# First head pair side by side in the opening, with two dummy products fewer: a linear-attention and bilinear-FFN kernel

## Chip, cores, metric

One core of one Trainium2 chip. The metric is the device time of the whole kernel in microseconds (us); one launch computes everything. Runs of this kernel come out at 322 to 324 us.

## The reference

Batch 8, 8 heads, 576 tokens, head width 64. Attention without softmax, an RMS norm over each head's 64 outputs, then an FFN on 4608 tokens with two up-projections that are multiplied:

```python
kv  = np.einsum('bhsd,bhse->bhde', k, v)          # one 64x64 matrix per head
out = np.einsum('bhsd,bhde->bhse', q, kv)
rms = np.sqrt(np.mean(out * out, axis=-1, keepdims=True) + 1e-06)
x   = (out / rms * g_norm)                         # -> [4608, 512]
y   = ((x @ w_a) * (x @ w_b)) @ w_out              # d_ff = 1536
```

## The kernel before

Eight batches of attention are woven into the FFN's strips of 512 tokens. Only batch 0's attention has no FFN to hide under: it is the opening, and it runs while the first weights are still being loaded. Heads go in pairs: head 2p on partitions 0 to 63 and head 2p+1 on 64 to 127 of each result. The 576 tokens are laid on 96 partitions, six tokens each (`EP, EC = 96, 6`).

The helpers for one pair (cuts marked with `# ...`):

```python
def kv(self, p, o):                       # 12 products, K = 96, 64x64 each
    for c in range(EC):
        for j in range(2):
            nc.tensor.matmul(
                o[j * D : (j + 1) * D, :],
                lhsT=kt[self.b % NB][:, 2 * p + j, c, :],
                rhs=vt[self.b % NB][:, 2 * p + j, c, :],
                start=(c == 0), stop=(c == EC - 1))

def qtr(self, p, i):                      # 12 transposes, 64 columns of weights each
    t = P[:, i, :].bitcast(BF16)[:, 0:S].rearrange("q (c t) -> q c t", c=EC)
    for c in range(EC):
        for j in range(2):
            nc.tensor.transpose(t[j * D : (j + 1) * D, c, :],
                                qt[self.b][:, 2 * p + j, c, :], ident[0:EP, 0:EP])
```

The opening. `dummy(n, i)` issues n products of zeros, 128x512, whose results nobody reads: they keep TensorE busy while the inputs land.

```python
A = Attn(0)
nc.vector.tensor_copy(qt[0][:, 0:2], q32)         # casts fp32 -> bf16 of the first pair
nc.scalar.copy(kt[0][:, 0:2], k32)
nc.vector.tensor_copy(vt[0][:, 0], v32[:, 0])
nc.scalar.copy(vt[0][:, 1], v32[:, 1])
dummy(11, 0)
A.qtr(0, 2); A.qtr_out(0, 2)                      # transposes of q, copy to SBUF
dummy(4, 7)
A.kv1(0, SS)                                      # the 12 products of kv
A.kv1_out(0, SS, nc.vector.tensor_copy)           # one 128x64 copy, PSUM -> kvs
A.qtr(1, 3); A.qtr_out(1, 3)                      # the second pair's transposes
nc.tensor.matmul(P[:, 1, 0:1], lhsT=g_row, rhs=one, start=True, stop=True)
# ...
A.px(0, X[0])                                     # q times kv, first pair
# ... the other pairs, then the first FFN products:
u0.first((0, 1))                                  # w_a, then w_b, of the first half of d_model
```

## Time and profile before

| | kernel before |
|---|---|
| time, three runs | 322.81, 323.08, 323.35 us |
| the profiled run | 324.26 us, span on the core 322.5 us |
| PE busy | 315.1 us, 98% of the span |
| opening on PE, first transposes to the first FFN product | 5.78 to 14.05 us |
| PE waits for the first piece of w_b | 1.05 us, until 15.71 us |
| PE waits for v of batch 2 | 1.00 us, until 61.20 us |

How to read the lines: the line numbers are those of the kernel; most are of helpers. In the kernel before L312 is a dummy, L164 a transpose, L140 a kv product, L178 `px`, L237 an FFN up-projection. In the changed kernel each of these is four higher, and L368, L372 and L381 are the new transposes, kv products and kvs copies. In e9 to e11 below each is one higher than before (L141, L238).

Busy time from the page of the kernel before (engine, us, share of the span, instructions):

```profile
PE 315.1 (98%) x1945; PEld 151.1 (47%) x1945; DVE 123.6 (38%) x214; ACT 125.3 (39%) x216; POOL 60.2 (19%) x82
```

PE's timeline in the opening of the kernel before (start us, duration us, engine, line, operation, weights' size, result size, count; in brackets the idle time ahead of it and what ended that):

```profile
5.78 0.45 PE L164 MATMUL P<-ident,qt 96*64 96x96 bf16 x12 [0.28 <-DVE qt L353]
6.16 1.04 PE L312 MATMUL P<-zeros 128*128 128x512 bf16 x4
7.13 0.38 PE L140 MATMUL P<-vt,kt 96*64 96x64 bf16 x12
7.34 0.42 PE L164 MATMUL P<-ident,qt 96*64 96x96 bf16 x12
7.69 0.38 PE L365 MATMUL P<-one,g_row 1*128 1x1 f32 x2
8.00 0.43 PE L178 MATMUL P<-qT,kvs 64*64 64x288 bf16 x4
...
14.05 0.60 PE L237 MATMUL P<-xt,wa_t 128*128 128x512 bf16 x2
15.71 0.60 PE L237 MATMUL P<-xt,wb_t 128*128 128x512 bf16 x2 [1.05 <-DMA wb_t<-in_moe_w_b_dram]
```

The 12 transposes, four dummies and 12 kv products follow each other from 5.78 us; the second pair's transposes start at 7.34 us. PE is done with the attention and the first two w_a products at 14.65 us and then has nothing to do until the first piece of w_b lands.

The second half of the cast of v, from ScalarE's timeline of the same run; it ends at 6.87 us, and kv of the second head can't begin before:

```profile
6.36 0.51 ACT L356 CAST vt<-v 96x384 bf16<-96x384 f32 x1
```

Two lines of PE's waits over the whole span (who waited for what: us in total, times, longest):

```profile
PE P L237 <- DMA wb_t<-in_moe_w_b_dram: 1.1, 1, 1.1
PE P L140 <- DMA vt<-in_v_dram: 1.0, 1, 1.0
```

And the second of them in the timeline, batch 2's 48 kv products:

```profile
61.20 0.95 PE L140 MATMUL P<-vt,kt 96*64 96x64 bf16 x48 [1.00 <-DMA vt<-in_v_dram]
```

### The profile page before, as it was taken

To read this page: it belongs to the slowest core of one execution; us is meant where nothing else is said; L and a number is where in the kernel's file an instruction comes from. 1 tells how busy PE (TensorE), PEld (TensorE's weight loads), DVE (VectorE), ACT (ScalarE), POOL (GpSimd) and SP (SyncE) were. 2 spreads that over 40 slices of the span, in tenths; PEclk is the share of its full clock that TensorE was granted. 3 is DMA by queue.
4 is the path that set the end of the run, shared out by engine and by line. 5 is a ranking of instruction groups with operands and counts; after the bars stand their busy time and mean duration, and the time that the engine had idled before them with its cause. 6 is when DMAs were issued, how large, how long until landed. Compare 5 with 4: busy or idle time off the path is not lost.

```text
span 322.5 us, 4835 instructions
## 1 busy us (share of the span) xinstructions
PE 315.1 (98%) x1945; PEld 151.1 (47%) x1945; DVE 123.6 (38%) x214; ACT 125.3 (39%) x216; POOL 60.2 (19%) x82
## 2 busy tenths in 40 slices
PE   8799999899999999999999999999999999999995
PEld 3344454444444444444444445444444444444443
DVE  3544335344244432543244333532355233313421
ACT  3542255354335434552355325533464233123310
POOL 8864870140032150320050000000000000000000
PEclk9999999999999999999999999999999999999999
DMA  8999999997359999496597142003000200020002
GB/s 180 197 196 200 192 173 236 140 116 117 91 103 151 143 143 226 57 154 131 138 102 122 52 97 56 2 33 99 2 0 0 100 33 0 17 95 23 0 35 98
DMA packets 69901, 32.61 MB, mean 101 GB/s; under 512 B 43638, under 2 KB 65398, under 8 KB 69878
## 3 DMA queue, kind: packets, MB, share of 16 engines
q0 software_dynamic: 49712, 18.44, 48.5%
q1 hardware_dynamic: 19810, 13.44, 16.8%
q10 hardware_dynamic: 356, 0.43, 0.4%
q8 instruction: 15, 0.25, 0.3%
q14 instruction: 8, 0.07, 0.1%
HBM read 37.75 MB, written 12.98 MB: 157 GB/s over the span
## 4 chain that ended last, share of the span: by engine, by line
PE 80%; DMA 14%; POOL 4%; issue 1%; ACT 0%; POOLq 0%
PE P L237 49%; PE P L287 26%; DMA wb_t<-in_moe_w_b_dram 6%; DMA vt<-in_v_dram 5%; PE P L217 2%; PE P L191 2%; DMA wo_t<-in_moe_w_out_dram 2%; PE P L140 2%; DMA qt<-in_q_dram 2%; POOL qs L122 1%; POOL kt L99 1%; POOL vt L99 1%; POOL qt L99 1%; POOL wa_t L340 0%; POOL wb_t L340 0%
## 5 line engine op out<-in xcount | busy, mean ns | idle before, releaser
L255 DVE TENSOR_TENSOR ab<-P,asb 128x512 bf16<-128x512 f32 x108 | 74.5, 692 | 125.4 <-PE P L237 124.4
L237 PE MATMUL P<-xt,wb_t 128*128 128x512 bf16 x432 | 111.7, 379 | 1.1 <-DMA wb_t<-in_moe_w_b_dram 1.1
L237 PE MATMUL P<-xt,wa_t 128*128 128x512 bf16 x432 | 111.9, 379 | 0.0
L287 PE MATMUL P<-wo_t,ab 128*128 128x512 bf16 (+1 forms) x444 | 97.9, 373 | 0.0
L251 ACT CAST asb<-P 128x512 bf16<-128x512 f32 x108 | 63.0, 585 | 81.8 <-PE P L237 80.3
L237 PEld LDWEIGHTS <-wb_t 128*128 128x128 bf16 x432 | 42.2, 98 | 52.2 <-DMA wb_t<-in_moe_w_b_dram 1.5
L287 PEld LDWEIGHTS <-ab 128*128 128x128 bf16 x444 | 43.1, 98 | 45.6
L237 PEld LDWEIGHTS <-wa_t 128*128 128x128 bf16 x432 | 41.7, 98 | 44.5 <-issue 0.5
L205 DVE SCALAR_TENSOR_TENSOR xt<-P,g_col,rs 128x288 bf16<-128x288 f32 x64 | 30.1, 513 | 25.4 <-ACT rs L195 25.4
L195 ACT ACTIVATE rs<-P,eps_t 128x576 f32<-128x576 f32 (+1 forms) x33 | 23.9, 726 | 22.4 <-PE P L191 18.4
L300 ACT COPY osb<-P 128x512 f32<-128x512 f32 x17 | 9.9, 585 | 48.6 <-PE P L287 46.8
L187 ACT ACTIVATE sq<-P 128x576 bf16<-128x576 f32 x31 | 20.1, 650 | 19.9 <-PE P L217 18.0
L302 DVE COPY osb<-P 128x512 f32<-128x512 f32 x18 | 12.5, 692 | 32.4 <-PE P L287 32.3
L122 POOL DMA_DIRECT2D qs<-in_q_dram x12 | 19.6, 1633 | 2.0 <-issue 1.9
L119 POOL COPY gate<-qT 1x1 bf16<-1x1 bf16 x5 | 0.9, 176 | 92.8 <-DMA qT<-qs 92.8
L191 PE MATMUL P<-sq,ones 128*128 128x288 bf16 x64 | 13.2, 286 | 0.5 <-ACT sq L187 0.4
L217 PE MATMUL P<-qT,kvb 128*128 128x288 bf16 x56 | 11.7, 286 | 0.0
L151 ACT CAST kvb<-P 64x256 bf16<-64x256 f32 (+1 forms) x20 | 6.0, 301 | 12.9 <-PE P L140 12.8
L191 PEld LDWEIGHTS <-ones 128*128 128x128 bf16 x64 | 6.2, 98 | 7.4 <-issue 0.4
L140 PE MATMUL P<-vt,kt 96*64 96x64 bf16 x384 | 8.6, 197 | 1.0 <-DMA vt<-in_v_dram 1.0
L140 PEld LDWEIGHTS <-kt 96*64 96x64 bf16 x384 | 7.3, 112 | 4.8 <-issue 4.4
L99 POOL DMA_DIRECT2D vt<-in_v_dram x13 | 9.1, 698 | 0.5 <-DMA qt<-in_q_dram 0.5
(41 smaller groups left out, 65.9 us busy)
## 6 DMA issues: line engine op xcount, KB each, us to landing
out_dram<-osb SPq DMA_DIRECT2D x23, 256.0 KB, 2.0
qs<-in_q_dram POOLq DMA_DIRECT2D x12, 288.0 KB, 6.4
kt<-in_k_dram POOLq DMA_DIRECT2D x6, 576.0 KB, 8.4
vt<-in_v_dram POOLq DMA_DIRECT2D x6, 576.0 KB, 11.1
out_dram<-osb SPq DMA_DIRECT2D x13, 128.0 KB, 2.3
wo_t<-in_moe_w_out_dram POOLq DMA_DIRECT2D x12, 128.0 KB, 6.0
wa_t<-in_moe_w_a_dram POOLq DMA_DIRECT2D x5, 256.0 KB, 9.1
wb_t<-in_moe_w_b_dram POOLq DMA_DIRECT2D x5, 256.0 KB, 8.8
```

The costliest lines, as they stand in the source:

```text
L99: nc.gpsimd.dma_start(out=t[:, hs, :, :], in_=src[b, hs].rearrange("h (t c) d -> t h c d", c=EC))
L122: nc.gpsimd.dma_start(out=d[:, hs, :], in_=q[b, hs].rearrange("h t d -> t h d"))
L140: nc.tensor.matmul(o[j * D : (j + 1) * D, :], lhsT=kt[self.b % NB][:, 2 * p + j, c, :], rhs=vt[self.b % NB][:, 2 * p + j, c, :], start=(c ...
L187: nc.scalar.activation(sq[p % 3], P[:, i0 : i0 + 2, 0:HF], AF.Square)
L191: nc.tensor.matmul(P[:, i0 + h, 0:HF], lhsT=ones, rhs=sq[p % 3][:, h, :], start=True, stop=True)
L195: nc.scalar.activation(rs[p % 3][:, h0:h1, :], P[:, i0 + h0 : i0 + h1, 0:HF], AF.Abs_reciprocal_sqrt, bias=eps_t,)
L205: nc.vector.scalar_tensor_tensor(out=xt[p][:, t0 : t0 + HF], in0=P[:, x0 + h, 0:HF], scalar=g_col, in1=rs[p % 3][:, h, :], op0=ALU.mult, o ...
L217: nc.tensor.matmul(P[:, i0 + h, 0:HF], lhsT=kvb[self.b % 2][:, p, :], rhs=self.qT[:, p, h * HF : (h + 1) * HF], start=True, stop=True,)
L237: nc.tensor.matmul(self.a if w is wa_t else self.b, lhsT=w[:, kc, self.fc * 128 : (self.fc + 1) * 128], rhs=xt[kc][:, t0 : t0 + STRIP], st ...
L251: nc.scalar.copy(self.t, self.a)
L255: nc.vector.tensor_mul(abt[self.s % 2][self.fc], self.b, self.t)
L287: nc.tensor.matmul(P[:, i, e0:e1], lhsT=abt[s % 2][fc][:, g * 128 : (g + 1) * 128], rhs=wo_t[:, fc, e0:e1], start=(fc == 0), stop=(fc == F ...
```

## The change

The intent: with the two heads side by side in the free dimension, one transpose and one kv product serve both heads, six instead of twelve of each, and two dummies that seem not to be needed are dropped. kv then yields a 128x128 result, of which only the two diagonal 64x64 blocks are wanted, so the copy to `kvs` becomes two copies.

```diff
+    qc = sb([EP, EC, 2 * D], BF16, "qc")
+    kc0 = sb([EP, EC, 2 * D], BF16, "kc0")
+    vc = sb([EP, EC, 2 * D], BF16, "vc")
 ...
-    nc.vector.tensor_copy(qt[0][:, 0:2], q32)
-    nc.scalar.copy(kt[0][:, 0:2], k32)
-    nc.vector.tensor_copy(vt[0][:, 0], v32[:, 0])
-    nc.scalar.copy(vt[0][:, 1], v32[:, 1])
-    dummy(11, 0)
-    A.qtr(0, 2)
+    nc.vector.tensor_copy(by_token(qc), q32)      # by_token: "p c (h d) -> p h c d"
+    nc.scalar.copy(by_token(kc0), k32)
+    nc.vector.tensor_copy(by_token(vc)[:, 0], v32[:, 0])
+    nc.scalar.copy(by_token(vc)[:, 1], v32[:, 1])
+    dummy(10, 0)
+    t = P[:, 2, :].bitcast(BF16)[:, 0:S].rearrange("q (c t) -> q c t", c=EC)
+    for c in range(EC):
+        nc.tensor.transpose(t[:, c, :], qc[:, c, :], ident[0:EP, 0:EP])
     A.qtr_out(0, 2)
-    dummy(4, 7)
-    A.kv1(0, SS)
-    A.kv1_out(0, SS, nc.vector.tensor_copy)
+    dummy(3, 7)
+    for c in range(EC):
+        nc.tensor.matmul(P[:, SS, 0 : 2 * D], lhsT=kc0[:, c, :], rhs=vc[:, c, :],
+                         start=(c == 0), stop=(c == EC - 1))
+    for j in range(2):
+        r = slice(j * D, (j + 1) * D)
+        nc.vector.tensor_copy(A.kvs[r, 0, :], P[r, SS, r])
```

More of the change, by code (lines that the diff above doesn't have):

```diff
@@ L352, with by_token @@
     A = Attn(0)
-    nc.vector.tensor_copy(qt[0][:, 0:2], q32)
-    nc.scalar.copy(kt[0][:, 0:2], k32)
-    nc.vector.tensor_copy(vt[0][:, 0], v32[:, 0])
-    nc.scalar.copy(vt[0][:, 1], v32[:, 1])
-    dummy(11, 0)
-    A.qtr(0, 2)
-    A.qtr_out(0, 2)
-    dummy(4, 7)
-    A.kv1(0, SS)
-    A.kv1_out(0, SS, nc.vector.tensor_copy)
+    def by_token(t):
+        return t.rearrange("p c (h d) -> p h c d", h=2)
+    nc.vector.tensor_copy(by_token(qc), q32)
[6 more added lines that the diff above has]
+        nc.tensor.transpose(t[:, c, :], qc[:, c, :], ident[0:EP, 0:EP])
+    A.qtr_out(0, 2)
+    dummy(3, 7)
+    for c in range(EC):
+        nc.tensor.matmul(
+            P[:, SS, 0 : 2 * D],
+            lhsT=kc0[:, c, :],
+            rhs=vc[:, c, :],
+            start=(c == 0),
+            stop=(c == EC - 1),
+        )
+    for j in range(2):
+        r = slice(j * D, (j + 1) * D)
+        nc.vector.tensor_copy(A.kvs[r, 0, :], P[r, SS, r])
     A.qtr(1, 3)
```

## The prediction

> **What bounds the kernel now.** TensorE. The page shows PE busy 98% of a 322.5 us span; from about 16 us on, the chain of waits is almost only FFN products (75% of the span on two lines). The change touches only the opening. In the timeline, PE waits for the cast of q until 5.78 us, runs batch 0's attention until 14.65 us, then idles 1.05 us, until 15.71 us, for the first piece of w_b (view of waits: "PE <- DMA wb_t 1.1, 1 time"). POOL issued that piece at 8.55 us. The stretches table shows the DMA engines saturated from 4 us on (about 200 GB/s), and POOL's issues depend on nothing that PE computes. After 15.71 us PE has no wait of note. So 15.71 us is set by transfers, not by the attention.
>
> **What the change does, costed.**
> - First pair's transposes: 12 of 64 columns become 6 of 128. The 12 held PE from 5.78 to 6.16, about 32 ns each. They already ran in two column halves; I estimate 0.25 to 0.36 us for the 6: saved 0 to 0.13 us.
> - First pair's kv: 12 products of 64x64 become 6 of 128x128. The 12 took 7.13 to 7.34, about 18 ns each. At the pace of the 512-column products (0.216 us, so 54 ns for 128) the six take 0.32 us: lost about 0.1 us. The Trainium skill ("TensorEngine Tiling (Array Packing)", Tile-to-Partition Mapping, restrictions) says column tiling disables fast weight load; the trace agrees in direction: a 64-column load lasts 112 ns, a 128-column one 98 ns. Loads overlap products, so I expect little from it.
> - kvs copy: one of 128x64 (0.23 us) becomes two of 64x64 on DVE: an estimated 0.15 to 0.2 us more, partly under the second pair's transposes.
> - Casts of q, k, v write with heads interleaved, same element counts: I expect the same 0.56, 0.83, 0.41, 0.51 us.
> - Two dummies fewer. The eleventh ran while PE waited for q's cast anyway: saved 0. The fourth after the transposes ended near 7.02 and delayed kv to 7.13; v's cast was done at 6.87, so kv may start near 6.93: saved 0.2 us.
> The order on DVE, ACT, POOL and SP is otherwise unchanged.
>
> **On the critical path.** In sum the attention ends 0 to 0.3 us earlier. PE then waits that much longer for w_b: 1.05 us becomes 1.1 to 1.4, still ending at 15.7 us. Expected gain: about 0 (I allow 0.1).
>
> **Prediction: 323.0 us, range 322.5 to 323.6.** Chances: faster by over 2% 0.005, within 2% 0.985, slower by over 2% 0.01.
>
> **What would show each step.** Right: first transposes at about 5.8 us; kv at 6.9 to 7.0; two kvs copies near 7.3 to 7.7; the first product with wb_t at 15.7 +-0.3 us after a longer idle time; from there the same distance to the end. Wrong: that product moves with the attention, or PE has no wait for w_b there.
>
> **What would make it wrong.**
> - The PE clock. Dummies start every 0.43 us until about 4.7 us and every 0.22 us after, though the granted clock reads 1.00 throughout. The Trainium skill ("TensorE: Matmul & The Clock Gate", Part 1) says full rate comes after about 3.4 us of sustained work in a free-running window; the trace agrees (work began at 1.19 us). A dummy fewer leaves PE idle from about 5.1 to 5.8 us. If full rate then came a window later, the opening would be over 1 us longer, exceed the 1.05 us of slack and cost up to 1.5 us.
> - Transfers landing earlier or later: DVE's casts run beside POOL's descriptor writing, and another access pattern might delay an issue; 0.2 us either way.

## More of the kernel before

Later batches are slotted between FFN units. In strip s = 1, batch 2's kv (48 products, four pairs) comes right after the unit n = 4:

```python
k0, kn, xs = (4, 1, (6, 9, 11, 13)) if s < 3 else (2, 1, (4, 7, 10, 12))
if k0 <= n < k0 + kn:
    for p in range(...):
        A.kv(p, kb[:, p, :])
```

Its k and v come through POOL's DMA queue, behind all weights and all inputs of batches 0 and 1.

## The result, and the profile after

The changed kernel took 323.04 us (median of 6 runs, 322.83 to 324.19), the kernel before on the same chip 322.94 (322.50 to 323.73, counting its three runs above). The ratio is 1.0009, with a 95% interval of 0.9988 to 1.003: the same. (Ratios here and below are the mean time of one kernel's fast runs over that of the other's of the same rounds, so not quite the ratio of the medians quoted.)

PE's timeline in the opening of the changed kernel:

```profile
5.78 0.43 PE L368 MATMUL P<-ident,qc 96*128 96x96 bf16 x6
6.06 0.81 PE L316 MATMUL P<-zeros 128*128 128x512 bf16 x3
6.97 0.49 PE L372 MATMUL P<-vc,kc 96*128 96x128 bf16 x6
7.39 0.45 PE L168 MATMUL P<-ident,qt 96*64 96x96 bf16 x12
7.77 0.38 PE L384 MATMUL P<-one,g_row 1*128 1x1 f32 x2
8.08 0.43 PE L182 MATMUL P<-qT,kvs 64*64 64x288 bf16 x4
...
14.35 0.38 PE L241 MATMUL P<-xt,wa_t 128*128 128x512 bf16 x1 [0.16 <-issue]
14.57 0.59 PE L241 MATMUL P<-xt,wb_t 128*128 128x512 bf16 x2
```

The six transposes are done by 6.06 us instead of 6.16, and kv starts at 6.97 instead of 7.13. But the six kv products hold PE for 0.42 us (6.97 to 7.39), where the twelve had taken 0.21 (7.13 to 7.34). The second pair's transposes start 0.05 us later than before. And the first product with w_b has no wait in front of it: it starts at 14.57 us. (The first of the two w_a products is missing from this trace's records; so are a few per cent of all matmuls.)

The second half of v's cast, and the two kvs copies on VectorE:

```profile
6.41 0.51 ACT L364 CAST vc<-v 96x384 bf16<-96x384 f32 x1
```

```profile
7.50 0.48 DVE L381 CAST kvs<-P 64x64 bf16<-64x64 f32 x2 [0.37 <-PE P L372]
```

v's cast ends at 6.92 us, and kv starts 0.05 us after that: it is now v that kv waits for. The copies end at 7.98 us, ahead of `px` at 8.08, which follows the product with g_row in PE's order either way.

The only line with a DMA in PE's waits of the changed kernel, and the same wait in the timeline:

```profile
PE P L144 <- DMA vt<-in_v_dram: 0.4, 1, 0.4
```

```profile
59.82 0.95 PE L144 MATMUL P<-vt,kt 96*64 96x64 bf16 x48 [0.40 <-DMA vt<-in_v_dram]
```

So the 1.4 us by which the span of this profile is shorter (321.1 against 322.5 us) lie ahead of these products, in transfers. What ends the wait there is the landing of v of batch 2, that is, the moment its data is there: about 61.1 us before, 59.8 us after (issued at 46.1 and 45.8 us, 15.0 and 14.0 us on the way). The late piece of w_b only made PE arrive later at the same wait: without it PE would have waited longer for v. From the start of the 48 products to the end it is 261.3 us in both (322.5 - 61.20 and 321.1 - 59.82). The timed runs show no such gain of 1.4 us. Was it luck of the profiled run, or the change?

### The profile page after: what moved, and what is told of

It reads as the page before. It is cut to its first block, busy times and chain, and to the rows that moved or that the text cites. A ratio compares the mean times of both kernels' runs of the same rounds, so it can differ in the third digit from the quotient of the medians.

```text
span 321.1 us, 4773 instructions
## 1 busy us (share of the span) xinstructions
PE 313.3 (98%) x1896; PEld 151.2 (47%) x1931; DVE 123.9 (39%) x215; ACT 125.3 (39%) x216; POOL 60.3 (19%) x82
## 4 chain that ended last, share of the span: by engine, by line
PE 80%; DMA 13%; POOL 4%; issue 1%; ACT 0%; POOLq 0%
PE P L241 49%; PE P L291 26%; DMA wb_t<-in_moe_w_b_dram 6%; DMA vt<-in_v_dram 4%; PE P L221 2%; PE P L195 2%; DMA qt<-in_q_dram 2%; PE P L144 2%; DMA wo_t<-in_moe_w_out_dram 2%; POOL qs L126 1%; POOL kt L103 1%; POOL vt L103 1%; POOL wo_t L118 0%; POOL wa_t L344 0%; POOL wb_t L344 0%
## 5 line engine op out<-in xcount | busy, mean ns | idle before, releaser
L241 PE MATMUL P<-xt,wb_t 128*128 128x512 bf16 x419 | 110.0, 379 | 0.4
L291 PEld LDWEIGHTS <-ab 128*128 128x128 bf16 x444 | 43.1, 98 | 45.6
L103 POOL DMA_DIRECT2D kt<-in_k_dram x13 | 9.2, 705 | 0.1
```

The lines of the kernel that those rows point to most:

```text
L103: nc.gpsimd.dma_start(out=t[:, hs, :, :], in_=src[b, hs].rearrange("h (t c) d -> t h c d", c=EC))
L241: nc.tensor.matmul(self.a if w is wa_t else self.b, lhsT=w[:, kc, self.fc * 128 : (self.fc + 1) * 128], rhs=xt[kc][:, t0 : t0 + STRIP], st ...
L291: nc.tensor.matmul(P[:, i, e0:e1], lhsT=abt[s % 2][fc][:, g * 128 : (g + 1) * 128], rhs=wo_t[:, fc, e0:e1], start=(fc == 0), stop=(fc == F ...
```

## Experiments

Twelve kernels ran, in three calls of four; all twelve gave correct results. The theories that the expectations below name:

- T (later T2, when it named the place): the landing times of transfers (when their data is there) vary from run to run whatever the kernel; runs differ by how long PE waits for them, above all for v of batch 2, and whatever the opening gains or loses disappears there.
- C: the change itself made w_b land earlier.
- R: the runs differ somewhere else.

The measured values in one table: time as median and range over all runs of that kernel, ratio to the kernel before in the same call, and from each kernel's profile the start of the first kv, of the second pair's transposes, of the first product with w_b, and the wait for v of batch 2 ("none": no such line).

| run | us (range) | ratio (95%) | kv | 2nd transp. | w_b | wait for v |
|---|---|---|---|---|---|---|
| before, profile above | 322.94 (322.50-323.73) | | 7.13 | 7.34 | 15.71 | 1.00 |
| after, profile above | 323.04 (322.83-324.19) | 1.0009 (0.9988-1.003) | 6.97 | 7.39 | 14.57 | 0.40 |
| e1_before_again | 323.20 (322.44-323.61) | 1.0008 (0.9996-1.002) | 7.14 | 7.35 | 14.59 | 1.12 |
| e2_after_again | 323.48 (322.63-326.14) | 1.003 (1.0003-1.0058) | 6.85 | 7.28 | 14.45 | 2.14 |
| e3_dummies_only | 323.31 (322.93-323.95) | 1.0016 (1.0003-1.0029) | 6.93 | 7.14 | 14.29 | 0.49 |
| e4_side_only | 323.28 (322.46-324.20) | 1.0012 (0.9996-1.0028) | 6.97 | 7.39 | 14.57 | 0.51 |
| e5_kv_later | 322.46 (322.16-322.98) | 0.9974 (0.9954-0.9995) | 7.12 | 7.33 | 15.47 | none |
| e6_after_kv_later | 322.32 (322.24-322.52) | 0.9973 (0.9955-0.9992) | 7.03 | 7.45 | 14.62 | none |
| e7_open_delay | 323.00 (322.87-324.25) | 1.0005 (0.9981-1.003) | 7.99 | 8.20 | 15.35 | none |
| e8_delay_kv_later | 322.89 (322.56-323.02) | 0.9989 (0.997-1.0008) | 8.03 | 8.23 | 15.39 | none |
| e9_transposes_only | 323.31 (322.85-324.16) | 0.9996 (0.9972-1.0019) | 6.72 | 7.05 | 14.21 | 0.52 |
| e10_hybrid | 323.06 (322.62-323.79) | 0.998 (0.9956-1.0004) | 6.82 | 7.02 | 14.19 | 1.49 |
| e11_hybrid_kv_later | 322.37 (322.23-322.45) | 0.9963 (0.9947-0.9979) | 6.84 | 7.02 | 14.20 | none |
| e12_kv_later_again | 322.36 (321.98-323.18) | 0.9967 (0.9948-0.9985) | 7.14 | 7.35 | 14.51 | none |

The kernel before, run beside each call, had medians of 322.75, 323.23 and 323.72 us in the three calls (the third on another chip). So times of different calls are compared by their ratios only.

### e1 and e2: both kernels once more

No edit: byte for byte the two kernels.

> The unchanged kernel before, run again against itself. In its one profile PE waited 1.05 us for the first piece of w_b (until 15.71 us) and 1.0 us for v of batch 2 (until 61.2 us); in the profile after both were near 0 and 0.4 us. Theory T (landing times of the transfers vary from run to run, whatever the kernel): here the wait for the first piece of w_b is anything from 0 to 1.1 us, most likely near 0, the time is 322.5 to 323.8 us as before, ratio 1.000 within 0.002. Theory C (the change itself made w_b land earlier): the wait is again 0.9 to 1.1 us and the first product with w_b again at 15.6 to 15.8 us. Both: second pair's transposes start at 7.34, first FFN product at 14.05 us, within 0.05.

> The changed kernel again. Theory T: time 322.8 to 324.2 us, ratio within 0.002 of 1; the first product with w_b anywhere from 14.5 to 15.8 us. Theory C: the first product with w_b again at 14.5 to 14.6 us, no wait. Both: second pair's transposes at 7.39, first FFN product at 14.12 to 14.35 us, that is 0.05 to 0.1 us later than before.

The unchanged kernel, profiled again, has no wait for w_b: its first product with it stands at 14.59 us. Theory C falls with that line. The first piece of w_b was late in 2 of the 14 profiles (before and e5, 1.05 and 0.82 us), and both have the kernel before's opening, but so do e1, e7, e8 and e12, where it was not late.

The first product with w_b in e1:

```profile
14.59 0.59 PE L237 MATMUL P<-xt,wb_t 128*128 128x512 bf16 x2
```

Batch 2's kv in e1 and then in e2:

```profile
60.52 0.95 PE L140 MATMUL P<-vt,kt 96*64 96x64 bf16 x48 [1.12 <-DMA vt<-in_v_dram]
```

```profile
61.39 0.95 PE L144 MATMUL P<-vt,kt 96*64 96x64 bf16 x48 [2.14 <-DMA vt<-in_v_dram]
```

The same two programs waited 1.00 and 1.12 us (before), 0.40 and 2.14 us (after). In e2 the wait had a sequel. From its view of stretches (from and to in us, its length, then PE, PEld, DVE, ACT and POOL busy us with counts, the granted clock, the DMA share, GB/s):

```profile
62.00:63.00 1.00, 0.92 (x23) 0.59 (x19) 0.00 (x0) 0.61 (x2) 0.00 (x0) 0.84 0.42 91
63.00:64.00 1.00, 1.00 (x3) 0.30 (x2) 0.00 (x0) 0.28 (x2) 0.53 (x2) 0.50 0.06 16
64.00:65.00 1.00, 1.00 (x4) 0.43 (x3) 0.00 (x0) 0.42 (x1) 1.00 (x1) 0.50 0.00 0
65.00:66.00 1.00, 1.00 (x4) 0.33 (x3) 0.39 (x1) 0.00 (x0) 1.00 (x2) 0.50 0.03 8
```

The wait ends at 61.39 us, and PE runs the 48 narrow products; in the stretch from 62 us the granted clock falls, and it is 0.50 for the three microseconds after 63. From the start of the 48 products to the end e2 takes 263.0 us (324.4 - 61.39) instead of 261.3: the wait cost 2.1 us and the clock another 1.7 (the shares of the clock missing in 62 to 67 us add up to the same: 0.16 + 3 x 0.50 + 0.05). That is the run of 326.14 us. Waits of up to 1.49 us (e10) left the clock at 1.00.

e2's ratio of 1.003 excludes 1.0, but the kernel before against itself in the same call gave 1.0008 (0.9996 to 1.002), so the kernel before's eleven runs of that call were on the lucky side; without the one run of 326.14 e2's mean is 323.40 us against e1's 323.12. I read no cost of the change from it. e2 missed its expectation in three points: the range of its times, the ratio (1.003 where 1.002 was the limit) and the start of the second pair's transposes, 7.28 instead of 7.39, because q was cast earlier in this run (transposes from 5.54 us; see the last section).

### e3 and e4: each half of the change alone

e3, the dummies only:

```diff
-    dummy(11, 0)
+    dummy(10, 0)
 ...
-    dummy(4, 7)
+    dummy(3, 7)
```

e4, the layout only: the changed kernel with `dummy(11, 0)` and `dummy(4, 7)` put back.

> Two dummies fewer, without the side-by-side layout. If the fourth dummy held kv up: kv starts at 6.95 +-0.04 instead of 7.13, the second pair's transposes at 7.16 instead of 7.34, and the first FFN product at 13.85 to 13.95 instead of 14.05. If something else held kv (v's cast at 6.87 with a longer delay): kv again at 7.13. Time: if the opening sets the time, ratio 0.9994 (0.18 us less), below what five rounds can resolve; if the transfers set it, 1.000. If the PE clock came late with a dummy fewer, dummies after the transposes would be 0.43 us apart in the trace and the time over 0.5 us longer; not expected.

> The side-by-side layout with all 15 dummies. Transposes 5.78 to 6.06 (as after), four dummies, so kv starts at about 7.02 to 7.18; six products take 0.42 us (as after; 12 narrow ones 0.21), so the second pair's transposes start at 7.45 to 7.6 and the first FFN product at 14.15 to 14.5, the latest of the four kernels. Time ratio 1.000 to 1.001.

PE's timeline of e3:

```profile
6.18 0.82 PE L312 MATMUL P<-zeros 128*128 128x512 bf16 x3
6.93 0.38 PE L140 MATMUL P<-vt,kt 96*64 96x64 bf16 x12
7.14 0.42 PE L164 MATMUL P<-ident,qt 96*64 96x96 bf16 x12
```

and of e4:

```profile
6.97 0.49 PE L372 MATMUL P<-vc,kc 96*128 96x128 bf16 x6
7.39 0.45 PE L168 MATMUL P<-ident,qt 96*64 96x96 bf16 x12
```

e3 does what it was expected to do: kv starts 0.20 us earlier than before, and so does all that follows on PE up to the second pair. e4 missed its expectation: with four dummies kv starts at the same 6.97 us as with three, not at 7.02 to 7.18. So in the changed kernel the dropped dummy is worth nothing (v's cast ends at 6.92 us in both), and in the kernel before it is worth 0.20.

Why does kv start earlier in e4 than before, with the same four dummies? The starts of single products, found by counting the instructions in windows that grow by 0.01 us, show it:

```
before, transposes   5.78 5.78 | 5.84 5.85 | 5.89 5.89 | 5.93 5.93 | 5.97 5.98 | 6.01 6.02
before, dummies      6.16  6.38  6.60  6.81
before, kv           7.12 7.13 | 7.18 7.18 | 7.21 7.21 | 7.24 7.24 | 7.27 7.27 | 7.30 7.31
before, 2nd transp.  7.33 7.34 | 7.38 7.38 | ...
after, transposes    5.78  5.84  5.88  5.92  5.97  6.01
after, dummies       6.05  6.27  6.49
after, kv            6.96  7.02  7.07  7.13  7.18  7.24
after, 2nd transp.   7.39 7.39 | 7.46 7.46 | ...
```

Three things are to be seen.

1. The narrow products already ran in pairs: the two heads start within 0.01 us of each other. Six pairs of transposes go at the same 0.04 us as six wide ones, so putting the heads side by side saves no PE time there. The Trainium skill ("TensorE: Matmul & The Clock Gate", Part 3) says that small products in separate tiles of the array run at the same time, their starts about 4 ns apart; the trace agrees as far as its steps of 0.01 us can show.
2. For kv the wide form is worse. A pair streams 64 columns of v (0.03 us a pair); a wide product streams the 128 columns of both heads (0.054 us) and computes two blocks that are thrown away. At that pace six cost 0.32 us, where the six pairs took 0.21.
3. Each of the three changes between 64-column and 128-column products here costs about 0.1 us: from the last narrow transposes to the first dummy 0.14 us, where wide ones follow in 0.04; from the last dummy to narrow kv 0.31 to 0.32, where dummies follow each other in 0.22; from the last wide kv to the narrow transposes 0.15, where wide kv follow in 0.054. The Trainium skill ("TensorEngine Tiling (Array Packing)", Key Properties) says that changing the tiling mode drains TensorE; the trace fits it, with 0.09 to 0.10 us a change. The weight loads (engine PEld) fit too: behind each of the three changes the first load begins only with its product (6.16 and 7.13 us before, 7.39 after), where wide ones begin ahead of it (after: 6.01 for the dummy at 6.05, 6.89 for kv at 6.96). No run changed only this.

The change removes the switches around the first dummies and puts one behind kv. Its account in the opening: kv starts 0.16 us earlier (0.10 of it from the switch behind the transposes; v's cast allows no more), and kv takes 0.21 us longer (0.11 for the columns, 0.10 for the switch). In sum 0.05 us later, which is 7.39 against 7.34.

The 0.05 us is that of these two profiles. With the kernel before's opening (before, e1, e5, e12) the second pair's transposes start at 7.33 to 7.35 us, whether v's cast ended at 6.86 or at 6.96: the dummies hold kv there. With the changed opening (after, e2, e4, e6) they start 0.47 to 0.48 us after the end of v's cast, at 7.28 to 7.45 us. So the change also moved kv from the dummies to v's cast, which varies from run to run.

e3's time ratio of 1.0016 says slower although its opening is the earlier one, with an interval that excludes 1. Its profile shows nothing for it (a span of 321.2 us, and the wait for v 0.49 us). e1, the same program as the kernel before, gave half of that. The chance of which landings a run meets is not averaged out by five rounds, and I don't explain it further.

### e5 and e6: batch 2's kv one unit later

The edit, in the kernel before (e5) and in the changed kernel (e6). Nothing is loaded earlier; kv is only computed 1.73 us later, still ahead of its first use:

```diff
-k0, kn, xs = (4, 1, (6, 9, 11, 13)) if s < 3 else ...
+k0, kn, xs = (5 if s == 1 else 4, 1, (6, 9, 11, 13)) if s < 3 else ...
```

> The kernel before, with kv of batch 2 computed one unit of the FFN (1.73 us) later, so that PE meets the landing of v (59.8 to 61.4 us in six profiles) at about 61.1 us instead of 59.4. Theory T2 (the wait for v of batch 2, 0.4 to 2.1 us in six profiles, is where runs differ and where gains of the opening vanish): the wait at the 48 products falls to 0 to 0.3 us, the time by 0.4 to 1.0 us (ratio 0.997 to 0.999) and the spread of runs shrinks to about half. Rival R (the runs differ elsewhere; the wait only moves): another wait of the same size appears behind it, ratio 1.000 within 0.001.

> The changed kernel with the same shift. Theory T2: as for the kernel before with the shift, 0.4 to 1.0 us under the kernel before; the difference between the two shifted kernels is what the change is worth where nothing swallows it: the opening's first FFN product is 0.05 to 0.1 us later, so ratio of the two 1.0002, not to be told from 1. If the change has a hidden gain in the opening that the wait for v swallowed, this kernel is faster than the shifted kernel before by 0.2 to 0.4 us.

Batch 2's kv in e6:

```profile
60.97 0.95 PE L144 MATMUL P<-vt,kt 96*64 96x64 bf16 x48
```

No wait is left (v landed at 59.7 us), and none appears behind it. Both kernels are faster than the kernel before, 0.9974 and 0.9973, and e6's six runs lie within 0.28 us, where the kernel before's ten of the same call lie within 2.19. T2 holds, R falls. All 14 profiles agree: from the start of batch 2's kv to the end it is 261.3 us in the eight unshifted ones other than e2, and 259.5 to 259.6 us in the five shifted ones, which is one unit less. So apart from e2's clock the profiles differ only in when these products start, and the shift costs nothing behind them.

The fastest run of the kernel before in that call, 322.16 us, equals e5's fastest, so most of the gain is bad draws taken away. Not all: the unshifted profiles without extra dummies have a wait of 0.40 us at the least, and in the third call e12's fastest run is 0.61 us below the fastest of the kernel before.

And the change itself: e6 over e5 is 322.36 / 322.48 (means of the six runs) = 0.9996. With the largest source of variation gone, the change is worth nothing in either direction that these runs can tell.

### e7 and e8: the opening made longer on purpose

```diff
-    dummy(4, 7)
+    dummy(8, 7)
```

in the kernel before (e7) and in e5 (e8): 0.86 us more for PE ahead of the first kv.

> The kernel before with four more dummies ahead of the first kv: 0.86 us more on PE in the opening. Theory T2 (transfers decide): first FFN product about 0.86 us later (14.9 us), the wait for v of batch 2 shorter by as much (to 0 to 0.3 us), time longer by only 0 to 0.45 us, ratio 1.000 to 1.0014. Rival (the opening lies on the critical path in full): 0.86 us longer, ratio 1.0027.

> The same four dummies in the kernel with kv of batch 2 later. Here T2 has no wait to swallow the delay except the one for the later pieces of w_b near 16.3 us (up to 0.15 us): 0.6 to 0.86 us longer than the shifted kernel without them (ratio of the two 1.002 to 1.0027). Rival (all of the opening is swallowed by other transfers): the same time as the shifted kernel.

Batch 2's kv in e7 and then in e8:

```profile
59.80 0.95 PE L140 MATMUL P<-vt,kt 96*64 96x64 bf16 x48
```

```profile
61.57 0.95 PE L140 MATMUL P<-vt,kt 96*64 96x64 bf16 x48
```

In e7 all of the delay is there at the first product with w_b (15.35 us, against 14.51 in e12's undisturbed opening), and the wait for v is gone: PE comes just as v lands. The time is 1.0005 of the kernel before: 0.86 us more work cost 0.07 us in the mean (323.30 against 323.23). What the delay does move is the fastest run, 322.87 against 322.16. In e8, where no wait for v swallows it, the delay costs 322.86 / 322.48 = 1.0012, or 0.38 us: visible, but less than the 0.6 to 0.86 that I expected. Against e6 it is 0.50 us. Part of the rest may be that e5 had a wait for w_b (0.82 us in the profiled run, 322.98 us) that a later opening doesn't meet. Part is, in the profiles, a third transfer, v of batch 1, shown under e11 and e12. So transfers ahead of v of batch 2 swallow some of the opening too, as the prediction said of w_b; how much falls to each, these runs don't separate.

### e9 to e12: the quicker of each kind, and where it goes

e9 takes only the wide transposes into the kernel before: `qc`, its cast, the six transposes; kv stays narrow, all 15 dummies. e10 is e9 with `dummy(10, 0)` and `dummy(3, 7)`. e11 is e10 with batch 2's kv later, e12 is e5 once more beside it.

> Only the transposes of the first pair side by side; kv stays in 12 narrow products, all 15 dummies. Additive account of the opening (from the profiles of before, after and the two half changes): six wide transposes take 0.28 us against 0.38, so kv starts at 6.97 to 7.03 instead of 7.13, the second pair's transposes at 7.17 to 7.24 instead of 7.34, the first product with w_a about 0.10 to 0.15 us earlier than before. Time ratio 1.000 within 0.0015 (the wait for v swallows it).

> The same with two dummies fewer: the wide transposes and the narrow kv, each the quicker of its kind. If v's cast (done at about 6.9) is what holds kv once a dummy or 0.1 us of transposes is gone, kv starts at 6.93 to 6.97, as with either alone, and the second pair's transposes at 7.14 to 7.18, 0.2 us ahead of before and 0.25 ahead of the change. If the dummies still held it, kv would start at 6.8. Time ratio 1.000 within 0.0015.

> The hybrid with kv of batch 2 one unit later. Theory T2: no wait for v of batch 2 (under 0.3 us), so the 0.2 us of the opening can reach the end, less what the later pieces of w_b take back near 16.3 us: 0 to 0.2 us under the shifted kernel before, ratio to the kernel before 0.996 to 0.9985, runs within 0.8 us of each other.

> The kernel before with kv of batch 2 later once more, on the same chip as the hybrid with the shift. Theory T2: again 0.4 to 1.0 us under the kernel before (ratio 0.997 to 0.999), runs within 0.9 us of each other. Rival: the earlier gain was that chip's luck, ratio 1.000.

e9's start times missed their range because q came earlier in that run: the transposes begin at 5.49 us instead of 5.78. From there to the second pair's transposes it is 1.56 us, as before (7.34 - 5.78): v's second half was cast at 6.82 us, so kv could not use the 0.1 us. In e10 and e11 v's cast ends at 6.79 us, kv starts at 6.82 and 6.84, and the second pair's transposes at 7.02: 0.23 us behind v's cast instead of 0.47. The expectation had put kv 0.1 us later because it took the cast's end from other profiles. This opening is the one that the change was after: on PE it is 0.3 us shorter up to the first FFN product.

What comes of these 0.3 us is to be seen in two lines each of e11 and, behind it, e12 (the first w_a products, and the product with the second piece of w_b):

```profile
13.76 0.60 PE L238 MATMUL P<-xt,wa_t 128*128 128x512 bf16 x2
...
16.41 0.39 PE L238 MATMUL P<-xt,wb_t 128*128 128x512 bf16 x1 [0.24 <-DMA wb_t<-in_moe_w_b_dram]
```

```profile
14.06 0.60 PE L237 MATMUL P<-xt,wa_t 128*128 128x512 bf16 x2
...
16.31 0.38 PE L237 MATMUL P<-xt,wb_t 128*128 128x512 bf16 x1
```

e11 is 0.30 us ahead at the first products and 0.10 us behind at the later one: it waits 0.24 us for the second piece of w_b, which landed at about 16.4 us; e9 and e10 wait for it there too (0.24 and 0.28 us). By batch 2's kv the two kernels stand at the same time, e11 first:

```profile
60.87 0.95 PE L141 MATMUL P<-vt,kt 96*64 96x64 bf16 x48
```

```profile
60.87 0.95 PE L140 MATMUL P<-vt,kt 96*64 96x64 bf16 x48
```

and both spans are 320.4 us.

At 35 us e11 was still 0.12 us behind, by the start of the down-projections, 35.35 against 35.23 us. The two come level at the first kv of batch 1, here in e11 and then in e12, each with the transposes ahead of it:

```profile
39.33 0.45 PE L165 MATMUL P<-ident,qt 96*64 96x96 bf16 x12
39.62 0.38 PE L141 MATMUL P<-vt,kt 96*64 96x64 bf16 x12
```

```profile
39.21 0.45 PE L164 MATMUL P<-ident,qt 96*64 96x96 bf16 x12
39.64 0.38 PE L140 MATMUL P<-vt,kt 96*64 96x64 bf16 x12
```

From the transposes to this kv it is 0.29 us in e11, and also in e8, which comes later (40.09 to 40.38). In e12 it is 0.43 us. The view of waits names no cause, but v of batch 1's first pair landed at about 39.6 us in both (issued at 34.37 us and 5.2 us on the way in e11, at 33.69 and 5.9 in e12), and in e1 too this kv (39.82) comes right behind the landing (39.7). So PE can't pass this place before 39.6 us: e12 itself loses 0.14 us there, and whatever more a shorter opening gains has a third transfer to wait for. It shows in the delay as well: of the 0.88 us by which e8 (one chip) is behind e12 (the other) at the first product with w_b, 0.74 are left at this kv and 0.70 at batch 2's.

Over all runs e11 is at 322.35 and e12 at 322.47 us in the mean, ratio 0.9996, with e12's runs spread wider (321.98 to 323.18, more than the 0.9 us expected) than e11's (322.23 to 322.45). So e12 confirms the shift on another chip (0.9967), and a shorter opening adds nothing that these runs can tell.

The version that beats both kernels is the shift of batch 2's kv, with any of these openings: 0.9963 to 0.9974 of the kernel before in four measurements whose intervals all exclude 1. It is 0.3%, about 1 us, mostly the bad draws. It was compared with the kernel before in the same calls, and with the changed kernel only across calls (322.32 to 322.46 us against 323.04 and 323.48).

## Why the prediction was right, and where it was wrong

- **The time, 323.0 us, within 322.5 to 323.6:** right, 323.04. The number doesn't test the reason given for it: the opening came out no shorter, so there was no gain for a transfer to swallow, and the result alone would look the same without any wait.
- **"So 15.71 us is set by transfers", "the first product with wb_t at 15.7 +-0.3 us after a longer idle time":** wrong as a property of the kernel. It was a property of one run. The prediction named the sign of it ("PE has no wait for w_b there"), and that is what the profile after shows: 14.57 us, no wait. The unchanged kernel run again shows it too (14.59), and 12 of 14 profiles have no wait at the first piece. The mechanism, transfers that swallow the opening, stands, but at three other places: the second piece of w_b at about 16.4 us when the opening is shortened (0.24 us in e11), v of batch 1 at 39.6 us, and v of batch 2.
- **"After 15.71 us PE has no wait of note":** wrong by its own profile, which has the wait of 1.00 us for v of batch 2. I had looked at the waits of the first 25 us. It is the place that decides: e5, e6, e11 and e12, which have in common that they take it away, are the only kernels whose interval lies below 1, and e7 shows that 0.86 us of extra opening cost 0.07 us in the mean.
- **"In sum the attention ends 0 to 0.3 us earlier":** wrong, 0.05 us later at the second pair in the profiles of before and after. The mis-sized term is kv, "lost about 0.1 us", which measured 0.21. The pace of 54 ns per wide product was right; the change of width behind it, about 0.1 us, was missing from the sum. The same missing term explains why the transposes gained 0.10 us without being quicker.
- **"The fourth ... delayed kv to 7.13 ... saved 0.2 us":** true of the dummy alone (e3, 6.93). In the changed kernel it saves nothing (e4), because v's cast holds kv there. The two savings don't add.
- **kv start at 6.9 to 7.0:** right, 6.97. **kvs copies near 7.3 to 7.7:** 7.50 to 7.98, 0.48 us for two instead of 0.23 for one; longer than estimated, and off the path as predicted.
- **The clock:** the fear did not come true in the time. The moment of the full rate does vary: e6's transposes go at 0.08 us and its first dummy after them takes 0.30 us, so full rate came near 6.4 us instead of before 5 us (before, e2). e6's kv starts 0.06 us later than in the changed kernel's profile, but v's cast ends 0.05 us later there too (6.97 against 6.92), so no cost of the clock is to be seen. The costly clock event was another, after the wait for v in e2.

What stays open: why v of batch 2 takes 13.9 to 15.7 us from issue to landing, and why the first piece of w_b was late twice; whether a wait of 2 us always lowers the clock (it happened in the one profile that had such a wait); and the ratios of e2 and e3 above 1.

## What to carry to other kernels

Before trusting a wait in one profile as the place where a gain will be absorbed, take the profile again, and look at the waits of the whole span and not only at the stretch that the change touches: here two waits of 1 us stood in the same list, one was luck, and the other decided the time. Putting two 64-wide operands side by side saved no PE time here, because the pair already ran in the two halves of the array; count streamed columns and changes of width, not instructions. When a late transfer meets a fixed point of the schedule, try moving its consumer back by one unit: here it was worth about 0.3%, where 0.3 us less work ahead of it was worth nothing that could be measured.

## What the Trainium skill lacked or had wrong

- "TensorE: Matmul & The Clock Gate", Part 1, has the clock fall to half after an idle window of about 3.4 us. Here an idle time of 2.14 us (e2) was followed by a fall to 0.50, some 1.3 us after PE had resumed with narrow products (an estimate from the 0.84 of the stretch 62 to 63), at a cost of 1.7 us; after 1.49 us (e10) it did not fall. It happened in one profile, and whether the narrow products count as idle there is not shown.
- "TensorEngine Tiling (Array Packing)", Key Properties, says that changing the tiling mode drains TensorE and gives no figure. Here a change between 64-column and 128-column products took 0.09 to 0.10 us more than the usual step.
- No page that I read says how far the landing of one and the same transfer varies from run to run. Here v of batch 2, issued between 45.6 and 46.1 us in all profiles, landed 13.9 to 15.7 us later, and with the consumer moved behind the landing the spread of the times fell from 2.19 to 0.82 and 0.28 us (e5, e6) and from 1.68 to 1.20 and 0.22 us (e12, e11).
- "SBUF — State Buffer", SBUF: two separate sides, says that GpSimd and a VectorE instruction in a two-port mode share a pair of ports, which the one that starts first keeps for its whole instruction while the other is blocked. The traces fit the blocking, but not the order as their start times show it: in e2 the cast of q took 0.56 us, and POOL's DMA issue, begun 0.19 us before it, took 0.88 instead of 0.63 us and ended 0.13 us after the cast; in e3 it was the cast that took 0.77 us. In the 14 profiles the casts begun at 4.87 and 4.92 us (e9, e2) ended at 5.43 and 5.48, with POOL's issue the long one; the twelve begun at 4.96 to 5.21 all ended at 5.72 to 5.77. No run tested the cause, nor that the cast is in such a mode. The page lacks the consequence that an opening jumps by a quarter of a microsecond (transposes at 5.54 and 5.78 us) on 0.04 us of difference in the start of that cast. VectorE's and POOL's lines of e2, then of e3:

```profile
4.92 0.56 DVE L361 CAST qc<-q 96x768 bf16<-96x768 f32 x1 [2.88 <-DMA q<-in_q_dram]
```

```profile
4.73 0.88 POOL L103 DMA_DIRECT2D vt<-in_v_dram  x1
```

```profile
4.96 0.77 DVE L353 CAST qt<-q 96x768 bf16<-96x768 f32 x1 [2.92 <-DMA q<-in_q_dram]
```

```profile
4.71 0.63 POOL L99 DMA_DIRECT2D vt<-in_v_dram  x1
```
